# The issue of an attention group's output store moved from SyncE's queue to ScalarE's

## The chip, the cores and the metric

The kernel runs on one core of one Trainium2 chip. The core has a TensorE for matrix products (PE in the profile, its weight loads PEld), a VectorE (DVE), a ScalarE (ACT), a GpSimd (POOL) and a SyncE (SP), each with its own queue of instructions, and 16 DMA engines that move data between HBM and the on-chip memories. An instruction that issues a transfer stands in the queue of the engine that issues it.

The metric is the time of one execution on the device in microseconds. The kernel before took 2308.41 us, the median of three runs (2302.83 to 2309.76).

## What is computed

A block with two branches over x of 2048 tokens by 1024 channels, all in float32. Six rows of modulation come from a small conditioning vector. The first branch is attention with a compressed memory over four segments of 512 tokens, 32 heads of 32 channels; the second is an MLP across the tokens.

```python
x = A_x
mod = (_silu(c) @ w_mod).reshape(c.shape[0], 6, 1, -1)
sa, ca, ga, sb, cb, gb = (mod[:, 0], mod[:, 1], mod[:, 2], mod[:, 3], mod[:, 4], mod[:, 5])
h = _layernorm(x, axis=-1) * (1 + ca) + sa
x = x + ga * _A_ref(h, A_wq, A_wk, A_wv, A_wo, A_beta)
h = _layernorm(x, axis=-1) * (1 + cb) + sb
x = x + gb * _B_ref(h, B_w1, B_b1, B_w2, B_b2)
```

In the first branch, for each segment s of four:

```python
logits = jnp.einsum("bhqd,bhkd->bhqk", qs, ks) * scale + mask
p = _softmax(logits, axis=-1)
a_dot = jnp.einsum("bhqk,bhkd->bhqd", p, vs)
pq = phi(qs)
num = jnp.einsum("bhld,bhde->bhle", pq, M)
den = jnp.einsum("bhld,bhd->bhl", pq, z)[..., None] + 1e-6
o = g * (num / den) + (1.0 - g) * a_dot
pk = phi(ks)
M = M + jnp.einsum("bhld,bhle->bhde", pk, vs)
z = z + jnp.einsum("bhld->bhd", pk)
```

The outputs of all segments are put together and multiplied by wo.

## The kernel before

**Attention.** The 32 heads are taken in 8 groups of four (g), the 2048 tokens in four segments (seg). The list `its` has 32 items t, one for each pair of group and segment: first all groups over segments 0 and 1, then all groups over segments 2 and 3. Each item goes through these steps:

- `project(t, piece)` makes K, V and Q of the group for the segment (products at L193 and L201, from the normed input `h` and the weights `wv`, `wq`), splits each into a high and a low part (`sg`), and calls `stack`, which has three transfers for each head (L325, L326, L327, `sk<-sg`) put the parts on top of each other on the partitions. `project` for later items also fills PE's time while the other steps wait.
- `maxima(t, h)` makes the scores of a head once (L431), takes the row maxima on VectorE (L432), transposes them (L438), has ScalarE and VectorE make `nt` of them (L440, L441), and has four small transfers write them into the last two rows of the stacks of two heads (L445, `sk<-nt`).
- `scores(t, h)` makes the scores again, transposed, with the maxima now subtracted in the product (L466, L469, L472, L473, from `sk`), takes the exponential on ScalarE (L467, L470, L474, into `p`), masks on GpSimd (L477), and makes a high and a low half-precision part (`ph`, L479 on ScalarE, L481 on GpSimd). The score products share two PSUM banks with the tag "s2", each free again when its exponential is done.
- `values(t, h)` multiplies by the values (L495), divides and gates (L498 to L505), and collects the head in `am`. With the fourth head the item's output is complete. Four transposes on PE bring it into `ps` (L510), ScalarE copies it into the tile `ot` (L512), and a transfer of 256 KB stores `ot` into the DRAM tensor `oT` (L513). The tile `ot` has a single buffer, so the copy of the next item waits for this store.

The main loop runs over n, one head a step: scores of head n, maxima of head n + 3, values of head n - 1, a piece of a projection for head n + 8, and what was planned for that step. Such planned work includes the fetch and split of later weights (`rawv`, `rawq` at L151; their stores `wsp` at L174), the normed tokens of later segments (`gaw` at L604, `hT` at L246, read back as `h` at L310), modulation weights (`rawm`, L520) and the weights of the output projection (`wor` at L578, `wos` at L590).

**Behind it.** `out_proj(tt)` reads 128 tokens of all groups from `oT` (`otr<-oT`, L691), splits them (`ots`), multiplies by wo (L706) and goes on to the second norm. Its first tiles are worked while the last attention items run; token tile 8 is the first of segment 2, so it needs the store of the last group for that segment. Then come the two products of the MLP (`mix`, L798), which take the second half of the time.

**What sets the order.** Every transfer of the kernel is issued by SyncE (`SY.dma_start`), in one queue. The order in each engine's queue is not that of the text: the program is built with `schedule_with_timeline_sim=True`, so a planner that simulates the timeline chooses, when the program is built, which ready instruction comes next on each engine. The order is then fixed, and an instruction that waits holds all that stands behind it in its queue. Only some places are pinned by hand (`tc.issue_after`).

Of the kernel before, what the change touches and what calls it, by code (L numbers as in the profile page):

```python
# [19 lines left out]
NSEG, L = 4, 512  # L20
# [24 lines left out]
def attention_and_mlp(ctx, tc, x, wq, wkv, wo, beta, w1, b1, w2, b2, c, wm_a, wm_b, out):  # L45
    nc = tc.nc
    V, A, G, T, SY = nc.vector, nc.scalar, nc.gpsimd, nc.tensor, nc.sync

    dram = ctx.enter_context(tc.tile_pool(name="dram", bufs=1, space=DRAM))
    oT = dram.tile([NG, P, S], F32, name="oT")  # L50
# [24 lines left out]
    def bank(tag, bufs, name):  # L75
        return psum.tile([P, 512], F32, tag=tag, bufs=bufs, name=name)
# [406 lines left out]
    def values(t, h):  # L483
        pr, g, seg = its[t]
        d = st[t]
        am, ph = d["am"], d["ph", h]
        pv = bank("pv", 1, f"pv{t}_{h}").rearrange("p (a n) -> p a n", a=4)
        col = {0: lambda i: 128 * i, 1: lambda i: 512 + 128 * (i - 1), 2: lambda i: 1024 + 128 * (i - 2),
               3: lambda i: 896}
        n = 0  # L490
        for part, w in ((0, NV), (1, 65)):
            for i in range(4):
                for j in range(i + 1):
                    o = col[j](i)
                    T.matmul(pv[:, i, 0:w], ph[:, part, o:o + 128], d["vp"][:, j, h, 0:w], start=(n == 0),  # L495
                             stop=(n == 19), skip_group_check=True)
                    n += 1
        V.reciprocal(pv[:, :, 0], pv[:, :, 0])  # L498
        red = r_.tile([P, 4, 32], F32, tag="red", bufs=2, name=f"red{t}_{h}")
        V.tensor_reduce(red, pv[:, :, 1:97].rearrange("p a (c e) -> p a e c", c=3), axis=AX.X, op=ALU.add)  # L500
        ah = am[:, :, 32 * h:32 * h + 32]
        V.scalar_tensor_tensor(red if seg else ah, red, gate[:, 1, 4 * g + h:4 * g + h + 1],
                               pv[:, :, 0:1].to_broadcast([P, 4, 32]), op0=ALU.mult, op1=ALU.mult)
        if seg:
            G.tensor_tensor(ah, ah, red, op=ALU.add)  # L505
        if h < 3:
            return
        ps = bank("ms", 1, f"ops{t}")
        for i in range(4):
            T.transpose(ps[:, 128 * i:128 * i + 128], am[:, i], ident)  # L510
        ot = r_.tile([P, L], F32, tag="ot", bufs=1, name=f"ot{t}")
        A.copy(ot, ps)  # L512
        SY.dma_start(oT[g, :, L * seg:L * seg + L], ot)  # L513
        del st[t]

    mcol = const.tile([P, 4 * NK], F32, name="mcol")
# [104 lines left out]
    for n in range(-LEADS, 4 * NI + VL):  # L621
        at(scores, n)
        at(maxima, n + LEADS)
        at(values, n - VL)
        m = n + LEADP
        if 0 <= m + 4 < 4 * NI:
            t = (m + 4) // 4
            if its[t][:2] not in W:
                with tc.issue_after(last_sk[0, 3].ins):
                    load_w(its[t][1], its[t][0])  # L630
        if m >= 8:
            at(project, m)
        if 59 <= m < 67:
            seg, ct = 2 + (m - 59) // 4, 2 * ((m - 59) % 4)
            reload_h(seg, ct)
            reload_h(seg, ct + 1)
        if 4 * NI - 5 <= m < 4 * NI + 3:
            i = m - 4 * NI + 5
            for c in (2 * (i % 4), 2 * (i % 4) + 1):
                wop[c, i // 4] = new_page(f"wo{c}_{i // 4}")  # L640
                SY.dma_start(wop[c, i // 4].bitcast(F32), wos[c, i // 4])
        for f, engines in todo.pop(n, ()):
            with behind(n, engines):
                f()
# [356 lines left out]
```

## Time and profile before

| | |
|---|---|
| median of three runs | 2308.41 us |
| lowest and highest run | 2302.83 and 2309.76 us |
| profiled execution | 2305.58 us |
| its span, first to last instruction | 2303.9 us |
| mean granted TensorE clock | 0.983 |
| DMA traffic | 414.67 MB, mean 180 GB/s |
| stores of `ot` | 32 of 256 KB |

The profile is one execution. Busy times are those of an engine's own work; waits and the issuing of transfers are not counted as busy. A line such as "SPq L513 <- ACT ot L512: 98.5, 21, 12.7" says that an engine's queue stood in front of line 513 for 98.5 us in total, 21 times, 12.7 us at the longest, until ScalarE's work on tile `ot` at line 512 was done. In a timeline, a row has its start, its duration, the engine, the line, the operation, the tiles written and read, and in brackets how long the engine was idle before it and what ended that. The chain of work that ended last is followed back from the last instruction, at each step to what released it.

### The profile page before, as it was taken

The numbers are of one execution on the slowest core, as the hardware profiler recorded it, in microseconds if no ns is written. First come the engines' busy times: TensorE is split into PE (matmuls) and PEld (weight loads), VectorE is DVE, ScalarE is ACT, GpSimd is POOL, SyncE is SP. The second block draws the span as 40 slices with busy tenths as digits, with TensorE's granted clock in tenths as the row PEclk, the third lists the DMA queues.
The fourth block names the chain that finished last, engine by engine and source line by source line (L and its number), as shares of the span: only waits on it lengthen the run. The fifth ranks groups of instructions, "written<-read, shape, count | busy, mean of one in ns | idle before, by whom it ended". The sixth has DMA issues, their size and how long they took to land.

```text
span 2303.9 us, 38456 instructions
## 1 busy us (share of the span) xinstructions
PE 2232.7 (97%) x13866; PEld 1918.9 (83%) x13866; DVE 1703.9 (74%) x3814; ACT 1105.6 (48%) x2018; POOL 727.9 (32%) x835
## 2 busy tenths in 40 slices
PE   8989999998999999999999999999999999999999
PEld 7879888898998889977787888888887888888877
DVE  5666666775777777657988665688889787878787
ACT  5477766755656656654324333543334242424232
POOL 3165655655666767653001000023333000000000
PEclk9989999999999999989999999999999999999999
DMA  6656555677566566663466664556557441414133
GB/s 256 199 164 183 173 162 162 195 247 225 156 199 206 166 189 187 202 212 112 137 205 213 249 237 181 202 222 239 206 201 263 171 151 55 151 55 142 55 119 146
DMA packets 172593, 414.67 MB, mean 180 GB/s; under 512 B 17236, under 2 KB 71540, under 8 KB 163444
## 3 DMA queue, kind: packets, MB, share of 16 engines
q1 hardware_dynamic: 172404, 412.22, 54.7%
q8 instruction: 110, 1.80, 0.3%
q14 instruction: 79, 0.65, 0.1%
HBM read 236.23 MB, written 125.06 MB: 157 GB/s over the span
## 4 chain that ended last, share of the span: by engine, by line
PE 81%; DVE 9%; DMA 5%; ACT 2%; issue 1%; POOL 1%; SPq 0%; DVEq 0%; ACTq 0%
PE mx L798 41%; PE nps L193 14%; PE qps L201 7%; PE po L706 6%; PE pv L495 3%; DMA wr<-in_w_dram 1%; PE a L466 1%; PE sx L431 1%; DVE ac L805 1%; PE sz L431 1%; DVE bU L123 1%; PE rd L403 1%; DVE sp L123 1%; DMA sk<-nt 1%; PE a L469 1%
## 5 line engine op out<-in xcount | busy, mean ns | idle before, releaser
L798 PE MATMUL mx<-bU,sp 128*128 128x512 f32 x2352 | 537.0, 390 | 4.7 <-DVE ac L805 2.0
L798 PEld LDWEIGHTS mx<-bU,sp 128*128 128x128 f32 x2352 | 440.4, 188 | 100.8 <-DVE sp L123 2.7
L193 PE MATMUL nps<-wv,h 128*128 128x256 f32 x3072 | 438.2, 284 | 0.7 <-DVE sg L123 0.5
L798 PE MATMUL mx<-bA,sp 128*128 128x512 f32 x1764 | 432.0, 390 | 2.5 <-DVE sp L123 2.2
L120 ACT CAST sp<-wr 128x384 fp32r<-128x384 f32 (+2 forms) x408 | 217.1, 545 | 449.9 <-PE mx L798 379.6
L481 POOL TENSOR_TENSOR ph<-p,ph 128x640 f16<-128x640 f32 x256 | 379.6, 1504 | 159.0 <-ACT ph L479 153.5
L193 PEld LDWEIGHTS nps<-wv,h 128*128 128x128 f32 x3072 | 403.8, 190 | 6.8 <-DVE sg L123 0.7
L798 PEld LDWEIGHTS mx<-bA,sp 128*128 128x128 f32 x1764 | 330.5, 188 | 73.5 <-DVE sp L123 2.9
L123 DVE TENSOR_TENSOR sp<-wr,sp 128x384 fp32r<-128x384 f32 (+2 forms) x408 | 256.8, 641 | 29.4 <-ACT sp L120 29.2
L805 DVE TENSOR_TENSOR ac<-mx,ac 128x512 f32<-128x512 f32 x280 | 189.3, 685 | 91.2 <-PE mx L798 90.5
L201 PE MATMUL qps<-h,wq 128*128 128x512 f32 x768 | 200.7, 406 | 1.4 <-DVE r L356 1.4
L432 DVE CUSTOM_DVE_ANT_0 sx<-sx,mask 128x128 f32<-128x128 f32 (+1 forms) x256 | 109.5, 428 | 113.6 <-PE sx L431 111.9
L706 PE MATMUL po<-wo,ots 128*128 128x512 f32 x768 | 184.8, 400 | 5.3 <-DVE x L709 3.1
L479 ACT CAST ph<-p 128x1280 f16<-128x1280 f32 x128 | 160.8, 1257 | 41.1 <-POOL p L477 40.3
L706 PEld LDWEIGHTS po<-wo,ots 128*128 128x128 f32 x768 | 148.3, 194 | 38.0 <-issue 3.9
L201 PEld LDWEIGHTS qps<-h,wq 128*128 128x128 f32 x768 | 144.4, 194 | 30.2 <-DVE r L356 1.2
L798 PE MATMUL mx<-bB,sp 128*128 128x512 f32 x588 | 164.3, 389 | 0.0
L477 POOL TENSOR_SCALAR_AFFINE_SELECT p<-p 128x256 f32<-128x256 f32 x256 | 120.5, 480 | 129.2 <-ACT p L470 63.4
L495 PE MATMUL pv<-vp,ph 128*128 128x97 bf16 (+1 forms) x2560 | 146.6, 204 | 5.5 <-DVE mv L134 2.7
L495 PEld LDWEIGHTS <-ph 128*128 128x128 f16 x2560 | 117.5, 100 | 29.4 <-issue 12.1
L805 DVE TENSOR_TENSOR cc<-mx,cc 128x512 f32<-128x512 f32 x140 | 94.6, 683 | 49.9 <-PE mx L798 45.4
L798 PEld LDWEIGHTS mx<-bB,sp 128*128 128x128 f32 x588 | 110.4, 188 | 23.4 <-ACT bB L120 0.6
(173 smaller groups left out, 3206.0 us busy)
## 6 DMA issues: line engine op xcount, KB each, us to landing
sk<-sg SPq DMA_DIRECT2D x384, 128.0 KB
wr<-in_w_dram SPq DMA_DIRECT2D x28, 1024.0 KB
wr<-in_w_dram SPq DMA_DIRECT2D x32, 768.0 KB
bstu<-ucd SPq DMA_DIRECT2D x28, 768.0 KB
wsp<-wv SPq DMA_DIRECT2D x32, 512.0 KB
rawm<-in_wm_b_dram SPq DMA_DIRECT2D x32, 512.0 KB
wv<-wsp SPq DMA_DIRECT2D x32, 512.0 KB
pcd<-cc SPq DMA_DIRECT2D x14, 1024.0 KB
```

The lines of the kernel that those rows point to most:

```text
L120: A.copy(hi, src)
L123: lo_eng.tensor_tensor(lo, src, hi.bitcast(F32), op=ALU.subtract)
L193: T.matmul(ps[:, aa], h[:, j, 128 * tt:128 * tt + 128], wt[:, i, o:o + 256], start=(n == 0), stop=(n >= 6 * NK - 2), skip_group_check=True)
L201: T.matmul(ps, wt[:, i, o:o + 128], h[:, j], start=(k + n == 0), stop=(3 * k + n == 3 * NK - 1))
L432: marks[4 * t + h - LEADS, "V"] = V.tensor_tensor_reduce(o, o, mask[:, 384 - 128 * i:], 1.0, -3.0e38, op0=ALU.add, op1=ALU.max, accum_out= ...
L477: G.affine_select(w, w, pattern=[[0, 2], [1, 128]], compare_op=ALU.is_ge, fill=0.0, base=0, channel_multiplier=-1)
L479: marks[n, "A"] = A.copy(ph[:, 0], p32)
L481: marks[n, "G"] = G.tensor_tensor(ph[:, 1, c], p32[:, c], ph[:, 0, c], op=ALU.subtract)
L495: T.matmul(pv[:, i, 0:w], ph[:, part, o:o + 128], d["vp"][:, j, h, 0:w], start=(n == 0), stop=(n == 19), skip_group_check=True)
L706: T.matmul(ps, os_[:, i, P * ct:P * ct + P], wop[ct, nh][:, j], start=(n == 0), stop=(n == 3 * NK - 1))
L798: T.matmul(ps, ops[q][:, i, P * k:P * k + P], b[:, j], start=(m == 0 and first), stop=(m == 3 * nk - 1), skip_group_check=True)
L805: V.tensor_tensor(d, ps, d, op=ALU.add)
```

## The change

The transfer that stores an item's output is issued by ScalarE instead of SyncE. It stands in ScalarE's queue, and so it waits there for the copy that fills `ot`, an instruction of the same engine. Its size, source and destination are the same. No other line differs.

```diff
         ot = r_.tile([P, L], F32, tag="ot", bufs=1, name=f"ot{t}")
         A.copy(ot, ps)
-        SY.dma_start(oT[g, :, L * seg:L * seg + L], ot)
+        A.dma_start(oT[g, :, L * seg:L * seg + L], ot)
         del st[t]
```

## The prediction

> **What bounds the kernel now.** I read the page first: the span, the busy times and the chain of work that ended last.
>
> ```profile
> span 2303.9 us, 38456 instructions
> PE 2232.7 (97%) x13866; PEld 1918.9 (83%) x13866; DVE 1703.9 (74%) x3814; ACT 1105.6 (48%) x2018; POOL 727.9 (32%) x835
> PE 81%; DVE 9%; DMA 5%; ACT 2%; issue 1%; POOL 1%; SPq 0%; DVEq 0%; ACTq 0%
> q1 hardware_dynamic: 172404, 412.22, 54.7%
> ```
>
> TensorE sets the time: 97% busy and 81% of the chain. ScalarE is 2% of it, SyncE's queue nothing. All program transfers go through one queue. Next, the rows of the edited tile show where the stores lie, and a table by stretch shows what that part looks like.
>
> ```profile
> L512 ACT COPY ot<-ops x32: 570/587/662, 151.0 to 1074.4; 128x512 f32<-128x512 f32 x32
> L513 SPq DMA_DIRECT2D oT<-ot x32: 319/326/1452, 151.6 to 1075.0; - x32
> L513 SPq EVENT_SEMAPHORE  x28: 17/17/17, 138.9 to 1038.7; - x28
> ```
>
> ```profile
> 150.00:1075.00 925.00, 890.63 (x7664) 806.45 (x7663) 638.02 (x1909) 589.36 (x1067) 575.61 (x683) 0.97 0.63 187
> ```
>
> The columns are span, then busy time of PE, PEld, DVE, ACT and POOL, granted clock, DMA share and GB/s. All 32 stores lie between 151 and 1075 us, in the attention. There PE is idle for 925.00 - 890.63 = 34.4 us, and a clock of 0.97 costs about 28 us more. These two, some 62 us, are all that better timing can win there. ACT is busy for 589.36 of 925 us, 64%. Last come the waits of that stretch, first SyncE's, then PE's.
>
> ```profile
> SPq L513 <- ACT ot L512: 98.5, 21, 12.7
> ...
> SPq L691 <- DMA oT<-ot: 2.0, 1, 2.0
> SPq L513 <- DMA h<-hT: 0.9, 1, 0.9
> SPq L513 <- DMA wor<-in_wo_dram: 0.7, 2, 0.3
> ```
>
> ```profile
> PE a L466 <- DMA sk<-nt: 8.2, 4, 2.8
> ...
> PE a L466 <- ACT p L474: 2.6, 2, 1.8
> ...
> PE po L706 <- ACT ots L120: 1.0, 1, 1.0
> ```
>
> SyncE stands 98.5 us in front of stores whose copy is not done. It looks like a large prize, but PE's waits for what SyncE carries (sk<-nt) are 8.2 us in four places.
>
> **What the change takes from SyncE.** It removes 32 issues of 0.33 us, 10.4 us, and the 98.5 us of waits. What that is worth depends on what stands behind the store. Two stretches show both answers.
>
> ```profile
> 178.96 0.34 SPq L604 DMA_DIRECT2D gaw<-in_x_dram  x1
> 182.34 0.33 SPq L513 DMA_DIRECT2D oT<-ot  x1
> 184.32 0.69 SPq L325 DMA_DIRECT2D sk<-sg  x1
> ```
>
> ```profile
> SPq L325 <- ACT nt L440: 2.0, 1, 2.0
> ```
>
> ```profile
> 841.65 2.62 SPq L445 DMA_DIRECT2D sk<-nt  x4
> 855.16 0.33 SPq L513 DMA_DIRECT2D oT<-ot  x1
> 855.59 0.37 SPq L520 DMA_DIRECT2D rawm<-in_wm_b_dram  x1
> 856.56 0.70 SPq L325 DMA_DIRECT2D sk<-sg  x1
> ```
>
> In the first, the store held SyncE until 182.34, but the stack behind it then waited another 2.0 us for a ScalarE result of its own, later in ScalarE's order than the copy. Without the store it starts at the same time. In the second, the store held SyncE for almost 11 us, and behind it came a weight fetch that nothing was short of; the stack behind that waited again. I therefore take a small gain: the 1.3 us that PE waits for an sk<-nt at 544 (below), in the stretch after the store that SyncE issued latest. The bounds are 0 and the whole 8.2 us.
>
> **What it adds to ScalarE.** ACT runs its instructions nearly without a seam; a store behind the copy puts one in. No row here has ACT issuing a transfer, so I price it from SyncE's rows.
>
> ```profile
> 330.68 0.61 ACT L512 COPY ot<-ops 128x512 f32<-128x512 f32 x1
> 331.15 0.63 ACT L474 ACTIVATE p<-a,shift 128x384 f32<-128x384 f32 x1
> ```
>
> ```profile
> 1048.61 0.59 ACT L512 COPY ot<-ops 128x512 f32<-128x512 f32 x1 [0.29 <-PE ops L510]
> ```
>
> ```profile
> 1049.23 0.32 SPq L513 DMA_DIRECT2D oT<-ot  x1
> 1051.58 0.37 SPq L691 DMA_DIRECT2D otr<-oT  x1
> ```
>
> The next activation starts 0.14 us before the copy ends. With the store between, ACT must see the copy end (the store at 1049.23 starts 0.03 us after the end at 1049.20), and issue (0.33): 0.14 + 0.03 + 0.33 = 0.50 us a store, 16.0 us in all. ACT has something to do at 64% of the places, so 10.2 us of that delays work. Little of ACT's lateness reaches PE: of PE's 34.4 us idle, the rows above give ACT 3.6, a tenth. But ACT also feeds POOL, DVE and the sk<-nt chain, so I take a quarter: 2.6 us. The bounds are 0 (an ACT that is never late for PE) and 16.0.
>
> The same rows also show that the last stretch doesn't change. The load at 1051.58 waits 2.0 us for the landing of the store just before it. That is a true dependence, and ACT issues that store at the same time as SyncE did.
>
> **The wait that moves onto ScalarE.** The store waits for more than its copy: 28 of 32 have an extra semaphore instruction, and three times the wait ended with the landing of a transfer that has nothing to do with it (h<-hT, wor). So some earlier transfer must have landed before a store may go. On SyncE such a wait is hidden in a queue that is late anyway. On ACT it would begin at the copy's end and hold everything behind it. How long is seen where SyncE issued the store late.
>
> ```profile
> 492.83 0.59 ACT L512 COPY ot<-ops 128x512 f32<-128x512 f32 x1 [3.69 <-PE ops L510]
> ```
>
> ```profile
> 496.72 0.66 SPq L513 DMA_DIRECT2D oT<-ot  x1
> ```
>
> ```profile
> 520.80 0.58 ACT L512 COPY ot<-ops 128x512 f32<-128x512 f32 x1
> ...
> 521.30 3.36 SPq L310 DMA_DIRECT2D h<-hT  x4
> ...
> 523.32 0.56 PE L466 MATMUL a<-sk 98*128 98x512 f32 x1 [1.85 <-DMA sk<-nt]
> ...
> 523.92 0.69 ACT L467 ACTIVATE p<-a,shift 128x512 f32<-128x512 f32 x1 [2.54 <-PE a L466]
> ...
> 527.76 0.27 ACT L440 ACTIVATE nt<-nmps 8x128 fp32r<-8x128 f32 x1 [2.08 <-PE nmps L438]
> ...
> 528.16 0.19 PEld L472 LDWEIGHTS a<-sk 98*128 98x128 f32 x1
> 528.25 0.32 SPq L513 DMA_DIRECT2D oT<-ot  x1
> ```
>
> ```profile
> 523.56:526.98 3.42, 3.42 (x14) 3.13 (x14) 1.50 (x6) 1.75 (x3) 1.63 (x3) 0.50 0.95 347
> ```
>
> ```profile
> 544.69 0.50 PE L466 MATMUL a<-sk 98*128 98x512 f32 x1 [1.32 <-DMA sk<-nt]
> ```
>
> At 521.38 the copy is done; the store goes at 528.25, 6.9 us later, behind four h loads, one of which had to land. If ACT inherits that wait, its L467 slips from 523.92 to about 528.6, by 4.7 us. PE runs on with projections until L472 at 528.16, which needs the bank that L467 empties, then stands about 1.1 us; L440 (527.76) comes some 3 us late, with it the next sk<-nt and the matmul that waits for it. PE thus loses between 1.1 and 4.7 us, and I take 3. The half clock that follows the PE gap before 523.32 lasted 3.42 us, so another such gap costs 1.7 more: 4.7. At 493.42 the store was 3.3 us late; a share of that and of smaller places gives 1.2. Bounds: 0, if the store on ACT draws no such wait, and 6.9 + 3.3 + 1.7 = 11.9.
>
> **Sum.** 2.6 + 4.7 + 1.2 - 1.3 = +7.2 us, slower. The profiled execution took 2305.58 us (its span is 2303.9), the median of the runs 2308.41; on the median the forecast is 2316.
>
> **A rule against the change.** All transfers of the program share one queue and 54.7% of 16 engines (first fence). The Trainium skill, "DMA: Bandwidth & Descriptors", section "Issuing engines are not separate DMA queues", says that transfers issued from several engines run on the same 16 and that spreading saves only the issuing time. By it, nothing is gained but 10.4 us of SyncE, which PE does not wait for, and the sum would be 8.5, 2317.
>
> **The rivals.** *SyncE set free (faster).* Every stack behind a held store goes earlier, PE's four waits for sk<-nt (8.2 us) vanish, and so does one half-clock stretch behind them (1.7): 2308.4 - 9.9 = 2298. For it speaks the 98.5 us; against it, the second wait at 184.32 and the fetch at 855.59. It decides once the stacks behind two of PE's four sk<-nt waits are issued a microsecond earlier. The Trainium skill, "Perfetto Trace Analysis", section "DMA Optimizations", holds that giving inputs and outputs an engine each allows a more dynamic spread. By it, this rival would be the outcome; that the 98.5 us stood in front of a store agrees with it.
>
> *ScalarE becomes the late one.* If most stores draw a wait and the seams fall in the latency chain of scores, most of 16.0 + 10.2 (the two late stores) reaches PE, say two thirds, 17.5, with one half-clock stretch of 1.7: 2328. It decides from the point where a hold of ACT outlasts the projections that PE has queued. For it: ACT is 64% busy, feeds POOL, DVE and the sk<-nt chain. Against: PE has projections to fill with, and its waits for ACT are small now.
>
> *Nothing reaches PE.* ACT's idle 36% swallows the seams and the early store draws no wait: 2308.
>
> *The change is more than a move.* The order on each queue is laid down ahead by a planner, and one issue moved can redraw the order elsewhere. This can push to either side and can't be priced from this trace, except that it has at most the 62 us above to win. It widens the range.
>
> **How the numbers follow.** A measurement of this kernel can tell about 0.3%, 6.9 us, from no change: 2301.5 to 2315.3. The forecast has 0.42, own range 2307 to 2325 (0.14 within 0.3%, 0.28 slower). SyncE set free 0.29 (0.28 faster, 0.01 same). ScalarE late 0.19, slower. Nothing 0.10 (0.09 same, 0.01 slower). Together: faster 0.28, same 0.24, slower 0.48. The range reaches from a little below the fast rival's 2298 to a little above the late ScalarE's 2328: 2296 to 2336.
>
> **What would show it.** Right: 32 issues of about 0.33 us on ScalarE's queue from L513; the row of 98.5 us gone, with SyncE's waits for other ScalarE results grown in its place; in a few places ACT idle for microseconds behind ot until a foreign transfer lands; PE idle above 34.4 us between 150 and 1075; a second DMA queue. Wrong: PE idle below 34.4 us with fewer waits for sk<-nt (SyncE mattered), ACT's issue several times 0.33 us, or a difference that lies after 1130 us, where no store is.

## The result

The changed kernel took 2311.98 us, the median of 17 runs (2303.69 to 2318.23), the kernel before in the same comparison 2305.71 us (17 runs, 2300.03 to 2310.91). The ratio is 1.0024 [1.0014, 1.0033]: slower by 6.3 us by the medians, which is a real difference, though less than the 0.3% called no change above. The profiled execution took 2312.21 us.

The page of the changed kernel first: span, busy times, the chain of work that ended last, and the two queues that the program now has.

```profile
span 2310.5 us, 38455 instructions
PE 2233.7 (97%) x13866; PEld 1920.3 (83%) x13866; DVE 1706.3 (74%) x3814; ACT 1105.9 (48%) x2018; POOL 724.2 (31%) x835
PE 77%; DVE 10%; DMA 6%; ACT 3%; issue 2%; POOL 2%; SPq 1%; ACTq 0%; DVEq 0%; POOLq 0%
q1 hardware_dynamic: 167796, 403.83, 53.6%
q10 hardware_dynamic: 4608, 8.39, 1.0%
```

TensorE is still the bound. In the chain PE gave 4% of the span to waits for other engines and transfers. The stores (8.39 MB) are a queue of their own. Their rows, by form:

```profile
L512 ACT COPY ot<-ops x32: 573/587/651, 149.9 to 1076.5; 128x512 f32<-128x512 f32 x32
L513 ACTq DMA_DIRECT2D oT<-ot x32: 326/326/357, 150.6 to 1077.1; - x32
```

By the median, ScalarE issues a store in the same 326 ns as SyncE did. The extra semaphore instructions have moved along with the stores: SyncE had 28, ScalarE now has 21, as the view of line 513 shows.

```profile
L513 ACTq EVENT_SEMAPHORE  x21: 17/17/17, 179.2 to 1076.5; - x21
```

Now SyncE's waits between 150 and 1080 us, and PE's.

```profile
SPq L325 <- ACT p L467: 29.9, 9, 9.5
SPq L325 <- ACT nt L440: 28.5, 6, 14.2
SPq L445 <- ACT nt L440: 26.8, 9, 7.3
```

```profile
PE a L466 <- DMA sk<-nt: 6.4, 6, 2.1
PE sx L431 <- DVE mx L432: 4.2, 5, 2.9
PE po L706 <- DMA wo<-wos: 3.6, 1, 3.6
```

The 98.5 us row is gone, and SyncE stands in front of other ScalarE results in its place. PE's last row is new: it waits 3.6 us for weights of the output projection. A table by stretch shows where PE loses. First before, then after; columns as in the prediction.

```profile
150.00:875.00 725.00, 698.85 (x6123) 638.12 (x6122) 502.20 (x1506) 470.73 (x864) 452.13 (x529) 0.98 0.64 189
...
875.00:1010.00 135.00, 134.57 (x1177) 122.43 (x1176) 89.48 (x289) 85.85 (x151) 88.17 (x114) 1.00 0.65 194
1010.00:1075.00 65.00, 57.22 (x369) 45.90 (x368) 46.34 (x115) 32.77 (x52) 35.31 (x41) 0.82 0.47 154
```

```profile
150.00:875.00 725.00, 702.66 (x6167) 641.60 (x6165) 509.65 (x1525) 475.41 (x871) 454.15 (x539) 0.98 0.65 193
...
875.00:1010.00 135.00, 131.22 (x1131) 118.75 (x1130) 84.33 (x271) 83.41 (x146) 83.47 (x104) 0.99 0.59 171
1010.00:1075.00 65.00, 52.45 (x345) 41.07 (x344) 40.71 (x108) 29.42 (x47) 35.85 (x40) 0.82 0.45 151
```

PE is idle for 22.3 us up to 875 (26.2 before), then for 3.8 (0.4 before) and 12.5 (7.8 before). So the change gains 3.8 us first and loses 8.1 in the last 200 us of the attention, where only seven of its 32 stores lie. The loss is no hold of ScalarE. Two stretches of the changed kernel's timeline, ScalarE's rows:

```profile
328.55 0.61 ACT L512 COPY ot<-ops 128x512 f32<-128x512 f32 x1
329.01 0.63 ACT L474 ACTIVATE p<-a,shift 128x384 f32<-128x384 f32 x1
329.19 0.33 ACTq L513 DMA_DIRECT2D oT<-ot  x1
329.49 0.63 ACT L120 CAST sg<-kps 128x512 fp32r<-128x512 f32 x1
```

```profile
809.79 0.60 ACT L512 COPY ot<-ops 128x512 f32<-128x512 f32 x1
...
811.78 0.33 ACTq L513 DMA_DIRECT2D oT<-ot  x1
812.15 0.27 ACT L440 ACTIVATE nt<-nmps 8x128 fp32r<-8x128 f32 x1 [1.27 <-DMA rawm<-in_wm_b_dram]
```

In the first the planner has put an activation between the copy and the store, the store is issued while it runs, and the next cast starts 0.15 us before the activation ends: no seam at all. For at least 19 of the 32 stores an instruction stands between and still runs when the store is issued. The second is the only place where a store is seen to wait for a foreign transfer: the cast `sg` that stands between ends at 810.88, the store goes at 811.78, a hold of 0.9 us. The planner has laid the order out anew on every queue. In the two orders that are recorded for the runs below, TensorE's queue has 16,170 instructions; the first 999 are the same, and a line comparison finds 2,120 in another place. That is the suspect that the experiments have to separate from the move.

### The profile page after: what moved, and what is told of

Same layout as the page of the kernel before. It is cut to its first block, busy times and chain, and to the rows that moved or that the text cites. A ratio compares the mean times of both kernels' runs of the same rounds, so it can differ in the third digit from the quotient of the medians.

```text
span 2310.5 us, 38455 instructions
## 1 busy us (share of the span) xinstructions
PE 2233.7 (97%) x13866; PEld 1920.3 (83%) x13866; DVE 1706.3 (74%) x3814; ACT 1105.9 (48%) x2018; POOL 724.2 (31%) x835
## 3 DMA queue, kind: packets, MB, share of 16 engines
q10 hardware_dynamic: 4608, 8.39, 1.0%
## 4 chain that ended last, share of the span: by engine, by line
PE 77%; DVE 10%; DMA 6%; ACT 3%; issue 2%; POOL 2%; SPq 1%; ACTq 0%; DVEq 0%; POOLq 0%
PE mx L798 41%; PE nps L193 11%; PE qps L201 8%; PE po L706 5%; PE pv L495 3%; DMA wr<-in_w_dram 1%; DVE ac L805 1%; PE a L466 1%; PE sx L431 1%; DVE bU L123 1%; DMA sk<-nt 1%; DMA x<-in_x_dram 1%; PE sz L431 1%; DVE sp L123 1%; DVE wv L123 1%
## 5 line engine op out<-in xcount | busy, mean ns | idle before, releaser
L495 PE MATMUL pv<-vp,ph 128*128 128x97 bf16 (+1 forms) x2560 | 146.2, 204 | 5.0 <-POOL ph L481 1.9
L495 PEld LDWEIGHTS <-ph 128*128 128x128 f16 x2560 | 116.4, 99 | 27.2 <-issue 7.9
```

## The experiments

To separate the two, a helper ties each queue to an order that was recorded from a built program. It adds a dependence for the order alone, with no semaphore:

```diff
+def pin(tc):
...
+    info = mybir.DependencyInfo(mybir.DependencyClass.NoSync, mybir.DependencyReason.DATA)
+    traced = {i.name: i for i in tc.nc.cur_bb.bb.instructions}
+    for text in ORDER:
+        nums = np.cumsum(np.frombuffer(zlib.decompress(base64.b85decode(text)), np.int32))
+        last = None
+        for n in nums.tolist():
+            i = traced.get(f"I-{n}")
+            if i is None:
+                continue
+            if last is not None:
+                tc.add_manual_dep(i, last.name, info, reason="pin")
+            last = i
...
         attention_and_mlp(ctx, tc, **args)
+        pin(tc)
```

The pinned experiments differ only in the line of the store and in the recorded order (`ORDER`, one text for each queue); the words behind `pin(tc)` below say which order it is and don't stand in the program. Ratios are to the kernel before on the same chip; an interval follows each.

### Before's order, store on ScalarE: the move alone

```diff
-        SY.dma_start(oT[g, :, L * seg:L * seg + L], ot)
+        A.dma_start(oT[g, :, L * seg:L * seg + L], ot)
...
+        pin(tc)   # before's order, each store right behind its copy on ScalarE
```

> The order of every queue is pinned to that of the kernel before; only the 32 stores stand on ScalarE's queue, each right behind its copy. Theory 'the move itself costs' (seams of 0.50 us on ScalarE and foreign landings that hold it): about +6 us, ratio near 1.0025, ScalarE held for microseconds at the copies near 493 and 521 us. Rival 'the redrawn order costs': ratio within 0.999 to 1.001, although the 98.5 us row of SyncE is gone.

Measured: 2309.19 us (12 runs), ratio 1.0007 [0.9996, 1.0019]. Here is the place that the prediction priced, in the timeline of this run:

```profile
521.52 0.58 ACT L512 COPY ot<-ops 128x512 f32<-128x512 f32 x1
...
524.02 0.47 PE L466 MATMUL a<-sk 98*128 98x512 f32 x1 [1.81 <-DMA sk<-nt]
...
529.18 0.33 ACTq L513 DMA_DIRECT2D oT<-ot  x1
529.56 0.69 ACT L467 ACTIVATE p<-a,shift 128x512 f32<-128x512 f32 x1 [7.46 <-DMA h<-hT]
...
530.30 0.33 PE L472 MATMUL a<-sk 98*128 98x128 f32 x1 [1.17 <-ACT p L467]
```

The copy ends at 522.10, the store goes at 529.18: ScalarE is held for 7.08 us behind a load of h, L467 slips to 529.56, and PE then stands 1.17 us at L472. All of this had been forecast (6.9; about 528.6; about 1.1). Three further holds are 0.94, 1.27 and 1.18 us. The other 28 stores start within 0.04 us of the copy's end, though 22 of the 32 have an extra semaphore instruction here: in most places the foreign transfer had landed by then. And only a fraction of these 10.5 us reaches the end. The stretch around the hold, in the kernel before and then in this run:

```profile
520.00:560.00 40.00, 34.19 (x287) 29.84 (x286) 21.92 (x70) 17.87 (x33) 19.21 (x23) 0.93 0.76 253
```

```profile
520.00:560.00 40.00, 34.63 (x289) 30.03 (x287) 21.49 (x67) 17.81 (x33) 19.23 (x24) 0.94 0.77 261
```

PE did as much in these 40 us with the hold as in the kernel before. There it waited 1.32 us for an sk<-nt at 544 (quoted in the prediction) and 1.81 us later on:

```profile
556.39 0.47 PE L466 MATMUL a<-sk 98*128 98x512 f32 x1 [1.81 <-ACT p L474]
```

With the hold neither of these waits is there: the lateness was for the most part spent in waits that stood there anyway. Against the 3.1 us saved stand the 1.17 us and 1.4 us more in front of L495 near 558 us (0.87 and 1.25 against 0.70). A single stretch proves little, though. The control below, with the same order, does more in it:

```profile
520.00:560.00 40.00, 36.59 (x294) 32.79 (x293) 23.19 (x67) 19.56 (x36) 20.91 (x25) 0.91 0.82 277
```

So two profiles of one order can differ by 2.4 us here, and the bound on what the move costs, seams and holds together, comes from the ratio.

### After's order, store on SyncE: the new order without the move

```diff
         SY.dma_start(oT[g, :, L * seg:L * seg + L], ot)
...
+        pin(tc)   # after's order, the stores put back into SyncE's queue
```

> The order of every queue is pinned to that of the changed kernel; only the 32 stores are issued by SyncE again, each at the place in its queue that its turn among all transfers gives it. Theory 'the move itself costs': back to the time before, ratio near 1.000. Rival 'the redrawn order costs': stays at the time of the changed kernel, ratio 1.0015 to 1.0035.

Measured: 2311.88 us (11 runs), ratio 1.0022 [1.0008, 1.0036]. SyncE's waits in this run:

```profile
SPq L513 <- ACT ot L512: 85.4, 21, 12.7
```

SyncE stands in front of the stores almost as long as in the kernel before, and the loss is the changed kernel's. The loss therefore comes with the order, not with the engine that issues.

### Control: before's order, store on SyncE

```diff
+        pin(tc)   # before's order, nothing moved
```

> Control: the order of every queue is pinned to that of the kernel before, and the stores stay on SyncE, so that the instructions are those of the kernel before. Both theories: ratio 1.000, within 0.001. A larger difference would be the noise of such a comparison.

Measured: 2305.83 us (12 runs), ratio 1.0000 [0.9986, 1.0015]. The helper itself costs nothing, and the two runs above can be read against the kernel before.

### Freeing SyncE without ScalarE, in two forms

In before's order, the stores stay on SyncE but stand further back, first eight transfers later:

```diff
 SyncE's queue, at each of the first 30 stores
-oT<-ot
 eight transfers
+oT<-ot
...
+        pin(tc)   # this order
```

> The order of the kernel before, pinned, with the stores on SyncE but the first 30 of them eight transfers later in its queue, so that SyncE hardly stands in front of a store any more and ScalarE is as before. Theory 'what stands behind a store waits for something of its own': the row of 98.5 us falls below 15 us and the ratio stays within 0.999 to 1.001. Rival 'SyncE set free': about -8 us, ratio 0.9965, PE's 8.2 us of waits for sk<-nt gone.

Measured: 2314.99 us (12 runs), ratio 1.0030 [1.0017, 1.0044]. SyncE's row for the stores and PE's row for the stacks in this run, each from its view of the waits:

```profile
SPq L513 <- ACT ot L512: 10.0, 1, 10.0
```

```profile
PE a L466 <- DMA sk<-nt: 11.8, 7, 2.9
```

The 98.5 us are down to one wait of 10.0 us. PE's waits for sk<-nt, which were to vanish, went from 8.2 us in four places to 11.8 in seven, and the kernel is slower. The profile is of an execution of 2306.75 us, 8 us below this run's median, so its waits can't account for the loss. One suspicion was that the late stores now stand among the stacks and delay them. So in the second form each store stands behind the next stacks, right ahead of a large transfer (3 to 28 transfers later):

```diff
 SyncE's queue, at each of the first 30 stores
-oT<-ot
 transfers up to the end of the next stacks
+oT<-ot
 the next large transfer
...
+        pin(tc)   # this order
```

> The order of the kernel before, pinned, stores on SyncE, the first 30 of them moved in its queue behind the stacks that follow, to just ahead of a bulk transfer (3 to 28 transfers later). Theory 'a store among the stacks delays them, SyncE's wait in front of it does not': the 98.5 us row gone, PE's wait for sk<-nt back at 8 us from 11.8, ratio 0.999 to 1.001. Rival 'SyncE running ahead is itself the harm': ratio near 1.003 again.

Measured: 2315.22 us (10 runs), ratio 1.0030 [1.0019, 1.0042]. SyncE's row for the stores is one wait of 10.2 us. PE's row in this run, whose profile is of its slowest execution (2318.47 us):

```profile
PE a L466 <- DMA sk<-nt: 16.8, 8, 3.5
```

The suspicion fell: the ratio is the same, and the waits for sk<-nt did not go back to 8 us. This run shows a second effect too: once the copy into the single `ot` buffer had to wait 4.3 us for a store put too far back. What may remain is that a SyncE without the stop at the store sends large fetches earlier, and that the small stack writes behind them are late. That was not isolated, and the move alone, which frees SyncE as much, cost only 1.0007. No form of freeing SyncE gained anything.

### Which part of the new order loses

The 25th store in before's order (at 883 us) cuts the work in two. One run has before's order up to it and after's behind, the other the reverse. In both SyncE issues the stores.

```diff
+        pin(tc)   # before's order for what before works up to the 25th store, after's for the rest
```

> Stores on SyncE. Every queue keeps the order of the kernel before up to the 25th store (near 883 us) and has that of the changed kernel behind it. Theory 'the redrawn order loses time in its last part': the profiles put 8 us more between the 25th and the last store and 3 more up to the end of the output projection, so ratio 1.003 to 1.005. Rival 'the loss lies spread over the whole order': half of it, ratio near 1.001.

Measured: 2316.7 us (9 runs), ratio 1.0036 [1.0022, 1.0050].

```diff
+        pin(tc)   # after's order for what before works up to the 25th store, before's for the rest
```

> Stores on SyncE. The order of the changed kernel up to the 25th store, that of the kernel before behind it. Theory 'the redrawn order loses time in its last part': its first part was 1.4 to 6 us ahead in two profiles, so ratio 0.9975 to 0.9995, faster than both kernels. Rival 'the loss lies spread': ratio near 1.001.

Measured: 2304.54 us (12 runs), ratio 0.9986 [0.9975, 0.9997], a little faster than both kernels. The two stretches of the first table, in the first of these runs and then in the second:

```profile
875.00:1010.00 135.00, 131.82 (x1167) 119.94 (x1164) 90.47 (x283) 85.18 (x153) 87.46 (x111) 1.00 0.63 188
1010.00:1075.00 65.00, 54.86 (x352) 43.66 (x349) 41.43 (x117) 32.45 (x51) 39.29 (x44) 0.76 0.49 154
```

```profile
875.00:1010.00 135.00, 135.00 (x1168) 122.57 (x1168) 86.09 (x284) 83.21 (x146) 82.49 (x105) 1.00 0.62 180
1010.00:1075.00 65.00, 56.26 (x356) 44.99 (x356) 47.10 (x115) 33.36 (x54) 35.25 (x40) 0.82 0.47 156
```

With after's last part PE is idle 3.2 and 10.1 us, and the clock is down to 0.76 in the second stretch; with before's last part 0 and 8.7 us. By the ratios the whole loss is in the last part of the redrawn order; its first part is, if anything, better than before's. (Each of the two runs joins two plans and so is a third order, which makes the split an approximate one.) One thing that differs in the last part is a late transfer. SyncE's issues of the second eight weight transfers `wo<-wos`, in the kernel before:

```profile
992.48 5.60 SPq L641 DMA_DIRECT2D wo<-wos  x8
```

and in the changed kernel, with PE's rows of the same time:

```profile
991.38 5.17 SPq L641 DMA_DIRECT2D wo<-wos  x7
...
1011.89 1.14 PE L706 MATMUL po<-wo,ots 128*128 128x512 f32 x4
1012.99 0.58 SPq L641 DMA_DIRECT2D wo<-wos  x1
1016.64 1.04 PE L706 MATMUL po<-wo,ots 128*128 128x512 f32 x3 [3.62 <-DMA wo<-wos]
```

The planner left one of the eight until 16 us after the other seven, and PE stands 3.62 us for it. The same wait is in the run with after's order and SyncE's stores (2.90 us) and in the run with after's last part (2.43 us). By itself it does not decide the time, though. Of the two runs with half of the stores moved, further below, the one as fast as before has such a wait too (2.1 us), and the one that is slower does not have it.

### Is it SyncE's order or the compute's?

```diff
+        pin(tc)   # before's order; behind the 25th store after's on PE, DVE, ACT and POOL; SyncE all before's
```

> Before's order on every queue up to the 25th store; behind it the changed kernel's order on TensorE, VectorE, ScalarE and GpSimd, and before's order on SyncE; stores on SyncE. The run with the changed kernel's order on all queues behind the 25th store had the ratio 1.0036. Theory A (the redrawn order of the transfers loses the time there, wo<-wos landing late at about 1013 to 1020 us): with SyncE's order restored the loss goes, ratio 0.999 to 1.001. Theory B (the redrawn order of the compute loses it): ratio 1.002 to 1.005, with PE gaps and half clock between 1030 and 1075 us. A split, 1.001 to 1.002, if both share in it.

Measured: 2330.53 us (6 runs), ratio 1.0092 [1.0063, 1.0122]. Neither theory expected that. The wait for wo<-wos is gone from PE's long waits, but others took its place:

```profile
1033.14 1.12 PE L510 MATMUL ops<-ident,am 128*128 128x128 f32 x4 [3.65 <-DVE nt L441]
...
1070.56 0.59 PE L495 MATMUL pv<-vp,ph 128*128 128x97 bf16 x10 [2.12 <-DVE red L502]
```

Restoring SyncE's order did not take the loss back: this mixture of two plans costs 21 us by the ratio, more than either plan. So the run does not tell the two theories apart. It stays open what in the last part of the new order loses the time; the compute order queue by queue was not tried.

### The better order with the move

```diff
-        SY.dma_start(oT[g, :, L * seg:L * seg + L], ot)
+        A.dma_start(oT[g, :, L * seg:L * seg + L], ot)
...
+        pin(tc)   # after's order up to the 25th store, then before's; store right behind its copy
```

> The changed kernel's order up to the 25th store, before's order behind it, each store on ScalarE right behind its copy. The same order with the stores on SyncE had the ratio 0.9986. Theory A (the move costs ScalarE some holds of 1 to 7 us, of which little passes on to TensorE): ratio 0.9986 to 1.000, that is 0 to 3 us above the one with the stores on SyncE, with one or more holds of over 0.9 us between a copy's end and its store. Theory B (the move itself gains once the order is good): ratio below 0.998. Theory C (holds reach TensorE): above 1.001.

Measured: 2305.69 us (11 runs), ratio 0.9994 [0.9979, 1.0010]. The same order with SyncE's stores had 0.9986, so the move adds 0.0008; in before's order it added 0.0007 (1.0007 against the control's 1.0000), and in after's order, where the planner had placed the stores, 0.0002 (1.0024 against 1.0022). That is 0.5 to 1.8 us, and each of the three differences lies inside its intervals: whether the move costs anything is not shown. This run has a single hold, of 0.5 us, at 810.73. The holds of over 0.9 us that were expected did not come.

### Other ways to make the planner draw anew

```diff
-        SY.dma_start(oT[g, :, L * seg:L * seg + L], ot)
+        with tc.high_priority():
+            SY.dma_start(oT[g, :, L * seg:L * seg + L], ot)
```

> Nothing is pinned or moved: the store stays on SyncE and is given a high priority in the planner, which redraws the order of all queues. Theory 'the redrawn order costs': a ratio that differs from 1 by 0.001 to 0.005, to either side, though the work and its engines are those of the kernel before. Rival 'a redraw costs nothing, the move does': ratio within 0.999 to 1.001.

Measured: 2305.89 us (12 runs), ratio 0.9991 [0.9978, 1.0004], with TensorE's rows in another order than before's: about half as many lines differ as between the profiles of before and after. Then half of the stores moved, the later half and the earlier half:

```diff
-        SY.dma_start(oT[g, :, L * seg:L * seg + L], ot)
+        (A if t >= 16 else SY).dma_start(oT[g, :, L * seg:L * seg + L], ot)
```

> Only the last 16 of the 32 stores issued by ScalarE, the planner free to place everything. Theory A (the time goes by the order that the planner happens to draw, not by how many stores are moved): anywhere from 0.998 to 1.004, with no relation to the 16 moved, and the difference in the part behind the 25th store. Theory B (each moved store costs): half of the changed kernel's excess, 1.001 to 1.0015.

Measured: 2313.54 us (11 runs), ratio 1.0029 [1.0015, 1.0043].

```diff
-        SY.dma_start(oT[g, :, L * seg:L * seg + L], ot)
+        (A if t < 16 else SY).dma_start(oT[g, :, L * seg:L * seg + L], ot)
```

> Only the first 16 of the 32 stores issued by ScalarE, the planner free. Theory A (the order that is drawn decides): anywhere from 0.998 to 1.004, and not together with the second-half run the sum of the changed kernel's excess. Theory B (each moved store costs): 1.001 to 1.0015.

Measured: 2306.02 us (12 runs), ratio 0.9998 [0.9982, 1.0014]. In the profile of the later half PE is busy for 51.66 of the 65 us from 1010 to 1075, at a clock of 0.76: the loss is again in the last part. The profile of the earlier half (an execution of 2309.33 us) looks no better there:

```profile
1010.00:1075.00 65.00, 51.77 (x332) 40.79 (x328) 39.52 (x106) 29.65 (x47) 34.25 (x40) 0.79 0.43 148
```

From 150 to 875 us, though, its PE has done 6,191 matmuls against 6,123 in the kernel before. In this execution the order gives up time in the last part too, and comes out about even because it is ahead by then. Sixteen moved stores cost as much as 32, or nothing. These redraws fit the order as the cause, but they don't prove it by themselves: a cost that only the later stores have would look the same. Against that stands the run with after's order and SyncE's stores, which has the loss with no store moved, and the run with the move alone, which has the later stores moved without it.

## Why the prediction was right or wrong

**The time.** 2316 was forecast, 7.2 us above before; it came out 6.3 above, slower, well inside the range. The measured 2311.98 is 4 us below the forecast, and the median of the kernel before came out 2.7 us lower in this comparison than in the first three runs. But the sum of that forecast is not what the 6.3 us consist of: that 7.2 and 6.3 lie so close is luck.

**Seams.** The size held. In the run with the move alone the store starts 0.03 us after its copy, takes 0.33, and in 16 of the 32 places the next instruction follows within 0.05; with the lost overlap of 0.14 us that is 0.55 there, against 0.50 forecast. In the others it comes 0.09 to 2.82 us after the store. In the changed kernel itself the planner avoided most seams, which the prediction had not thought of.

**The wait that moves onto ScalarE.** Its place, length and first effect on PE came out almost to the tenth when the order was held: 7.08 us for 6.9, 1.17 us at L472 for 1.1. What failed is the next step, that a late sk<-nt would bring PE's loss to 3 us and another half-clock stretch would add 1.7. In that profile PE's work over 40 us was no less than before, and two later waits of 3.1 us together were gone. In the changed kernel the planner moved this store so that the hold is not there at all; one of 0.9 us is left.

**The sum of the move.** The seams' 2.6 and the hold's 4.7 and 1.2 were 8.5 us, 7.2 with SyncE's gain. The move alone measures 0.0007 [-0.0004, 0.0019], 1.6 us with up to 4.4; the medians of this run and of the control lie 3.4 us apart. This is the term that was mis-sized: the share of ScalarE's lateness that reaches PE. How the cost divides into seams and holds, no run tells.

**SyncE set free.** The small gain of 1.3 us is not seen: with the move alone PE waits for sk<-nt 9.9 us in five places, in the control 8.6 in four. The rival that made the gain 9.9 us failed in three runs: 1.0007, 1.0030 and 1.0030, with the row of 98.5 us gone, at 10.0 and at 10.2. What the Trainium skill says may make sense ("Perfetto Trace Analysis", section "DMA Optimizations", an engine each for inputs and outputs) brought nothing here. The rule against the change ("DMA: Bandwidth & Descriptors", section "Issuing engines are not separate DMA queues") agrees with the move alone: what SyncE saves in issuing is not seen in the time.

**The change is more than a move.** This rival was right, and it had been given no chance and no price. It holds most of the 6.3 us: 1.0022 with the new order and no move, 1.0036 with its last part alone, 0.9986 with its first part alone. It could have been given a chance from the kernel's own text, since one planner orders every queue. Its sign could not be known from the trace: the runs in which the planner was free span 0.9991 to 1.0029.

**The signs that were named.** Right: the 32 issues of 0.33 us, the second queue, the 98.5 us gone with other waits for ScalarE in its place, PE idle above 34.4 us (38.7). The holds of microseconds are in the run with the move alone, not in the changed kernel. A sign of being wrong is there in part, a difference after 1130 us. The ends of the output projection and of the MLP, by form, before and then after:

```profile
L706 PE MATMUL po<-wo,ots x768: 387/389/795, 998.8 to 1220.1; 128*128 128x512 f32 x192
L798 PE MATMUL mx<-bU,sp x2352: 387/389/501, 1752.7 to 2299.1; 128*128 128x512 f32 x196
```

```profile
L706 PE MATMUL po<-wo,ots x768: 387/389/795, 997.2 to 1225.6; 128*128 128x512 f32 x192
L798 PE MATMUL mx<-bU,sp x2352: 387/389/504, 1760.3 to 2305.8; 128*128 128x512 f32 x196
```

The last store is 2.1 us later than before, the end of the output projection 5.5, the end of the MLP 6.7. No store lies there. In the run with after's order and SyncE's stores the output projection ends later still, which points to the order:

```profile
L706 PE MATMUL po<-wo,ots x768: 387/389/792, 1001.5 to 1229.7; 128*128 128x512 f32 x192
```

## What to carry to other kernels

Where a planner orders all queues, a one-line move is two changes: the move, and a new order everywhere. Price them apart, and when a small difference is to be explained, pin the order of one kernel and apply the move to it; the same order with and without the move is the only fair pair. A long wait of a queue that is off the critical path was no prize here, and the 7.08 us hold on ScalarE, an engine that is often idle, was mostly paid from waits that followed it.

## What the runs showed of the hardware

ScalarE's queue issues a 256 KB store in 326 ns by the median, as SyncE's does, 0.03 us after the copy that it follows. Most stores have an extra semaphore instruction on either queue: 28 of 32 on SyncE, 21 on ScalarE in the changed kernel, 22 in the run with the move alone. On ScalarE such a store can wait for a foreign transfer, up to 7.08 us here; 28 of the 32 in that run were not seen to. How much the order alone is worth was not expected: with the same work and the stores on SyncE, the orders tried here lie between 0.9986 and 1.0092.
